# Thirty-odd steps of the first batch's attention moved in a written-out order, and four matmul groups of the MLP put behind others

## The chip, the cores and the metric

The kernel runs on one core of a Trainium2 chip. The metric is the device time in microseconds (us) of one execution. Three runs of the kernel before took 256.25, 258.79 and 259.25 us; their median is 258.79.

## The reference

Four batches, eight heads, 768 positions, head size 64; everything comes and goes in float32. Attention lets a position see the four first positions (sinks) and the last 128. Its output, heads side by side, is `x` (768 rows of 512), which goes through a ResMLP:

```python
keep = is_sink | in_window                  # 4 sinks, window of 128
a = softmax(where(keep, q @ k.T / 8, -1e9))
x = concat_heads(a @ v)                     # [4, 768, 512]
tok = einsum('ts,bsd->btd', w_tok, alpha1 * x + beta1)
u = x + lam * tok
ch = relu((alpha2 * u + beta2) @ w_ch1) @ w_ch2      # 512 -> 2048 -> 512
out = u + lam * ch
```

## The kernel before, in words

The program is one list of 1143 small steps ("tasks"). `Plan.add` (L44) records each while the code walks through the batches; `Plan.emit` (L54) then writes out the instructions in the order that the tuple `ORDER` (L216) gives, by task number. The string `ENGINES` (L282) gives each task's engine (0 ACT, 1 DVE, 2 PE, 3 POOL, 4 SP), `HOMES` (L297) gives each buffer its slot, and `IDLES` (L307) puts some matmuls on zeros ahead of a few early PE tasks. So an engine does its tasks in the order in which they stand in `ORDER`, and a task waits for the data that it reads and for its slots to be free.

Batch 0's attention. Queries and keys come as head pairs: pair 0 in float32, cast by DVE; pairs 1 to 3 by POOL loads that cast to float16 on the way (`load_qk`, L390). PE turns them round (L504, L507), ACT or DVE copies them to `qkT`. PE makes scores (L617, L681), ACT their exponentials `E` (L639, L686), POOL or a bias on PE masks them, PE multiplies with the values (L718), and DVE normalises (L743, L744) into `x`. For batch 0 POOL multiplies `x` with alpha1 · lam (L753) into `xh`, which PE contracts with the transposed w_tok (`wtokT`, made from loads in the first microseconds by L816, L809 and copies at L155/L157) in L849; DVE adds the sum to `x` (L856), ACT or POOL casts it to `u16` (L155, L157). `fold_rows` (L1164, L1166) makes the rows alpha1 · lam and beta1 · lam (a product, then a shuffle that spreads it over partitions). Before that POOL makes small constant tiles: the masks (L333 to L341), `bm` (L354, L358, one 8-column tile for the sinks), the identity `iden` (L325, L326), and the selector with an 8×8 identity (`make_sel`, L365, L369), which the transpose of the alpha2 and beta2 rows (`abT`, L1168) needs.

The MLP. `uTp` (L890) turns two column blocks of three `u16` tiles round into a PSUM bank, and ACT or DVE scales them into `uT` (L873, L876). A group (`mlp1`, L929) is four matmuls of 128x128 by 128x384: one of 16 column blocks of w_ch1 for one half (three row blocks) of the batch; its result sits in one of four PSUM banks `d` until a relu frees it (ACT L935, DVE L937). The second matmuls follow (L1114; batches 1 to 3 by a Strassen-like scheme, L1046). The attention of the next batch is spread between these groups.

The weights. w_ch1 comes as four quarters by POOL loads with a cast (`load_w1`, L448), of four column blocks each; a group needs its quarter. After the second quarter has landed, SP may go on: it issues a tiny "gate" copy (L455) that waits for the quarter, and the loads behind it are w_ch2 (L444), keys and queries of batch 1 (L397) and values (L407). ACT issues some of these loads too. POOL or DVE folds w_ch2 with lam (L831).

Batch 0's groups stand in this order on PE, by task number: groups of the quarters at hand, then the last quarter's groups of half 0 (291, 289, 293, 295), with the two transposes `uTp` of half 1 (246, 241) between them, then three groups of an earlier quarter (257, 277, 259), then 267 and on.

Of the kernel before, what the change touches and what calls it, by code (L numbers as in the profile page):

```python
# [77 lines left out]
def kernel(  # L78
# [119 lines left out]
    for r in range(NR):  # L198
# [18 lines left out]
        26, 6, 9, 7, 10, 5, 11, 8, 18, 15, 72, 19, 1, 12, 3, 0, 4, 2, 22, 14, 73, 74, 45, 48, 46,  # L217
        17, 39, 49, 47, 53, 13, 40, 50, 41, 90, 95, 43, 91, 51, 54, 103, 52, 16, 44, 61, 104, 42,
        96, 109, 100, 62, 107, 110, 63, 55, 28, 108, 92, 56, 101, 21, 68, 65, 59, 93, 20, 69, 97,
        102, 111, 94, 24, 98, 57, 60, 30, 112, 105, 23, 58, 99, 113, 128, 106, 114, 116, 25, 131,  # L220
        135, 78, 115, 64, 27, 138, 31, 32, 117, 132, 29, 129, 136, 33, 122, 66, 125, 34, 123, 137,
        119, 139, 126, 35, 79, 70, 120, 140, 124, 84, 71, 80, 133, 130, 141, 67, 146, 85, 134, 121,
        147, 144, 75, 118, 158, 86, 154, 148, 159, 145, 142, 87, 149, 150, 155, 160, 143, 76, 88,
        151, 156, 81, 77, 166, 152, 162, 167, 89, 127, 82, 163, 213, 83, 168, 209, 164, 165, 214,
        210, 153, 217, 179, 211, 178, 157, 197, 229, 36, 212, 215, 218, 185, 216, 226, 230, 219,
        176, 161, 177, 220, 169, 223, 222, 232, 225, 224, 221, 227, 237, 233, 279, 238, 234, 228,
        273, 280, 182, 171, 204, 291, 274, 175, 289, 292, 200, 231, 293, 290, 246, 294, 295, 199,
        384, 241, 248, 188, 186, 257, 296, 247, 172, 243, 277, 174, 181, 242, 259, 258, 187, 170,
        278, 267, 37, 260, 271, 358, 268, 198, 285, 349, 272, 381, 301, 286, 366, 351, 303, 302,
        189, 297, 378, 173, 304, 281, 180, 352, 203, 249, 190, 282, 298, 379, 250, 287, 380, 192,  # L230
        353, 385, 288, 206, 283, 386, 369, 375, 367, 265, 284, 368, 202, 370, 266, 363, 376, 371,
        253, 377, 201, 299, 254, 372, 364, 183, 382, 191, 300, 373, 615, 365, 275, 374, 383, 357,
        261, 276, 408, 262, 387, 263, 184, 409, 205, 195, 239, 411, 264, 410, 395, 269, 396, 240,
        397, 270, 196, 388, 614, 621, 235, 412, 400, 194, 244, 398, 236, 401, 255, 617, 251, 245,
        256, 389, 390, 399, 252, 311, 359, 207, 193, 391, 424, 616, 335, 425, 393, 341, 426, 392,
        336, 648, 427, 634, 413, 394, 312, 636, 414, 428, 419, 404, 420, 415, 360, 405, 313, 429,
        208, 422, 337, 416, 361, 441, 421, 622, 402, 314, 423, 442, 626, 403, 305, 638, 315, 406,
        430, 640, 316, 435, 431, 306, 641, 355, 436, 443, 619, 437, 338, 649, 618, 438, 362, 317,
        432, 637, 407, 307, 433, 345, 444, 339, 439, 635, 318, 445, 450, 434, 639, 644, 319, 451,
        628, 452, 620, 440, 308, 645, 340, 453, 417, 446, 323, 447, 418, 320, 309, 448, 324, 321,  # L240
        658, 322, 329, 449, 642, 659, 454, 325, 625, 643, 330, 646, 347, 455, 326, 623, 343, 647,
        464, 344, 456, 465, 348, 466, 460, 457, 467, 650, 327, 458, 331, 461, 629, 459, 472, 462,
        632, 463, 653, 356, 651, 656, 627, 332, 38, 654, 480, 333, 342, 624, 652, 473, 310, 476,
        468, 471, 470, 469, 481, 474, 488, 885, 477, 475, 482, 492, 655, 490, 493, 350, 483, 478,
        514, 491, 516, 489, 657, 479, 515, 660, 517, 630, 882, 665, 518, 663, 354, 328, 666, 502,
        880, 661, 664, 498, 879, 519, 508, 499, 346, 503, 678, 662, 512, 509, 679, 504, 513, 487,
        484, 671, 485, 676, 486, 506, 677, 877, 548, 505, 672, 680, 507, 526, 549, 546, 527, 631,
        334, 522, 674, 681, 528, 547, 907, 523, 534, 903, 529, 633, 682, 675, 878, 542, 683, 535,
        890, 689, 543, 550, 685, 684, 690, 510, 551, 494, 511, 673, 667, 544, 495, 668, 891, 496,
        686, 545, 901, 687, 669, 497, 693, 888, 688, 883, 530, 694, 670, 700, 531, 524, 897, 701,  # L250
        698, 500, 691, 525, 696, 699, 552, 501, 697, 704, 553, 558, 695, 705, 904, 692, 562, 559,
        706, 909, 887, 707, 563, 564, 898, 708, 702, 566, 565, 910, 715, 703, 567, 532, 716, 889,
        713, 533, 709, 714, 896, 520, 710, 556, 717, 521, 538, 557, 537, 540, 539, 536, 560, 541,
        899, 718, 921, 572, 922, 881, 711, 574, 884, 573, 576, 712, 561, 719, 902, 577, 575, 555,
        727, 720, 569, 908, 721, 580, 728, 578, 722, 581, 729, 554, 723, 905, 730, 568, 739, 724,
        579, 725, 592, 570, 911, 726, 582, 740, 593, 588, 912, 583, 595, 584, 571, 906, 743, 589,
        731, 585, 900, 590, 732, 605, 744, 587, 733, 596, 606, 734, 607, 611, 594, 597, 602, 745,
        612, 586, 613, 599, 895, 603, 591, 757, 765, 600, 758, 601, 759, 766, 741, 771, 760, 742,
        916, 772, 751, 917, 746, 773, 752, 913, 761, 919, 774, 886, 767, 918, 604, 762, 763, 598,
        768, 777, 764, 779, 920, 923, 780, 914, 755, 915, 778, 608, 756, 926, 930, 735, 609, 931,  # L260
        924, 927, 781, 736, 925, 775, 782, 737, 928, 753, 929, 893, 738, 934, 754, 892, 769, 935,
        932, 610, 941, 770, 819, 776, 942, 894, 939, 820, 821, 940, 937, 936, 823, 749, 822, 945,
        748, 824, 938, 747, 827, 933, 948, 950, 750, 952, 943, 951, 825, 953, 787, 828, 944, 807,
        788, 797, 826, 808, 949, 946, 829, 798, 801, 954, 830, 791, 802, 956, 947, 792, 783, 955,
        957, 963, 961, 784, 789, 958, 962, 811, 790, 964, 959, 785, 812, 965, 805, 786, 795, 806,
        960, 967, 796, 799, 793, 968, 966, 970, 972, 794, 813, 971, 969, 815, 973, 814, 809, 800,
        816, 803, 810, 974, 978, 804, 976, 979, 837, 975, 977, 835, 838, 980, 841, 836, 839, 842,
        818, 843, 840, 845, 981, 832, 982, 846, 817, 986, 844, 831, 990, 987, 983, 988, 847, 991,
        984, 851, 833, 992, 1002, 993, 834, 848, 855, 852, 985, 849, 1003, 859, 856, 1004, 989,
        1006, 850, 860, 1005, 853, 998, 1007, 1008, 868, 999, 857, 1009, 997, 865, 995, 858, 862,  # L270
        996, 869, 866, 1000, 874, 994, 854, 1001, 1016, 863, 875, 1040, 1017, 1038, 1041, 1032,
        1039, 871, 1020, 872, 1028, 1021, 1011, 1024, 1029, 1013, 1018, 1033, 1012, 1025, 1034,
        1019, 1036, 1010, 1035, 1042, 1037, 1076, 1043, 1070, 1077, 870, 1074, 1071, 1054, 1075,
        1022, 1055, 1060, 1023, 1048, 1061, 1058, 1049, 1066, 1059, 1014, 1044, 1015, 1067, 1072,
        1045, 1056, 1073, 1026, 1057, 1078, 1068, 1079, 1064, 1069, 1046, 1027, 1050, 1063, 1047,
        1052, 1082, 1053, 1051, 1084, 1083, 1062, 1065, 1030, 1085, 1080, 1101, 1031, 1081, 1091,
        1102, 1107, 1092, 1097, 1093, 1103, 864, 1108, 1105, 867, 1098, 1111, 1106, 1104, 1113,
        1112, 1089, 1114, 1115, 1086, 1116, 1090, 861, 1094, 1087, 1117, 1099, 1109, 1100, 1121,
        1095, 1110, 1125, 1118, 1122, 1124, 1134, 1126, 1123, 1128, 1135, 1127, 1119, 1136, 1088,
        1140, 1120, 873, 876, 1131, 1129, 1141, 1096, 1137, 1142, 1132, 1130, 1133, 1138, 1139,  # L280
    )
    ENGINES = (  # L282
        "3313134433443333444444444444444433334441111201201202120212021213030121211201211210200200"
        "2020201202011202020202020213213213213213213202002020202020213121312131213121312131404444"
        "4044413314433334411114413334444042213221321021020121021021321202020020211212021212120212"
        "1212020202120202120212020212020202020212122221022221422221022221422221022221013111111131"
        "1311333333302002002102132002132002102020101212010321213120301212131201012121312010121213"
        "1203212131212131213421342104110121042104213401012020202021202020212120202020212120202121"
        "2121202111202021202120202011202121212121111121212121212121132111213121421021421421421044"
# [1033 lines left out]
```

The softmax here doesn't subtract the row's maximum and nothing guards it: scores larger than these inputs give would overflow.

## Time and profile before

| what | value |
|---|---|
| runs (us) | 256.25, 258.79, 259.25; median 258.79 |
| span of the profiled execution | 254.3 us, 5499 instructions |
| PE busy | 245.6 us, 97% of the span |
| DVE, ACT, POOL busy | 190.7, 133.2, 103.2 us |
| mean granted clock of PE | 0.997 |
| w_ch1 quarters issued by POOL at | 20.96, 21.77, 22.50, 23.23 us |
| landed at | 30.52, 35.95, 39.15, 43.40 us |

All times within a run are counted from the start of the profiled span. In a list of waits each line says which engine and which instruction waited, for whom, the total, how many times and the longest. In a timeline a line is: start, duration, engine, source line, operation, output and inputs, number of instructions, and in brackets the idle time just before and what ended it. "PEld" is the loading of weights, and an engine's name with a "q" its issuing part. The chain of waits is followed back from the last instruction to the first.

### The profile page before, as it was taken

What the parts mean: (1) busy time and instruction counts of PE and PEld (TensorE: products, weight loads), DVE (VectorE), ACT (ScalarE), POOL (GpSimd) and SP (SyncE); (2) the same over time, 40 slices, a digit from 0 to 9 for tenths busy, and PEclk for the clock granted to TensorE, in tenths of its full rate; (3) what the DMA queues carried; (4) which work ended last, traced back from release to release, by engine and by line L of the source; (5) the groups of instructions that cost most, each with busy time, mean ns of one, the idle gap of its engine ahead of it and who ended that gap; (6) DMA issues with size and microseconds to landing.
All of it is one profiled execution on the core that took longest, in us unless ns stands there. A gap on an engine that the chain in (4) does not pass through costs nothing.

```text
span 254.3 us, 5499 instructions
## 1 busy us (share of the span) xinstructions
PE 245.6 (97%) x2167; PEld 159.9 (63%) x2167; DVE 190.7 (75%) x402; ACT 133.2 (52%) x219; POOL 103.2 (41%) x124
## 2 busy tenths in 40 slices
PE   7799997999999999999999999999999999999993
PEld 7554644666555544566687686667667676667882
DVE  5688986767888874978879995578778983228892
ACT  2599913879977034787833434566660235543000
POOL 8318845876455527515782040065662120000010
PEclk9999999999999999999999999999999999999998
DMA  6999999899999999998484764520000140100327
GB/s 182 205 215 266 272 269 316 246 377 300 221 158 233 234 208 156 195 249 180 110 170 107 128 122 138 144 65 0 3 0 3 30 84 13 41 0 3 117 73 268
DMA packets 86129, 38.79 MB, mean 153 GB/s; under 512 B 73540, under 2 KB 80460, under 8 KB 86104
## 3 DMA queue, kind: packets, MB, share of 16 engines
q1 hardware_dynamic: 66576, 28.06, 47.3%
q10 hardware_dynamic: 15784, 7.11, 11.8%
q0 software_dynamic: 3744, 3.28, 8.0%
q8 instruction: 17, 0.28, 0.4%
q14 instruction: 8, 0.07, 0.1%
HBM read 29.91 MB, written 6.29 MB: 142 GB/s over the span
## 4 chain that ended last, share of the span: by engine, by line
PE 84%; DMA 11%; DVE 2%; POOL 1%; SPq 0%; issue 0%
PE h L929 32%; PE P L1046 22%; PE tok L849 9%; PE ch L1114 8%; DMA w1f<-in_moe_w_ch_dram 8%; PE pv L718 3%; PE S L617 3%; DMA nat<-in_k_dram 3%; PE tp L507 1%; POOL w1f L448 1%; PE tp L504 1%; DVE qkT L157 1%; DVE E L696 1%; PE pv L711 1%; PE pv L604 1%; PE idle L148 0%
## 5 line engine op out<-in xcount | busy, mean ns | idle before, releaser
L929 PE MATMUL h<-uT,w1f 128*128 128x384 f16 x512 | 89.8, 326 | 1.5 <-DMA w1f<-in_moe_w_ch_dram 1.5
L929 PEld LDWEIGHTS <-w1f 128*128 128x128 f16 x512 | 48.2, 98 | 32.7 <-DMA w1f<-in_moe_w_ch_dram 1.9
L935 ACT ACTIVATE hT<-h 128x384 f16<-128x384 f32 x77 | 37.0, 491 | 39.5 <-PE h L929 39.3
L937 DVE TENSOR_SCALAR hT<-h 128x384 f16<-128x384 f32 x51 | 27.8, 555 | 23.4 <-PE h L929 22.8
L1046 PEld LDWEIGHTS <-hT 128*128 128x128 f16 x408 | 39.5, 98 | 6.7 <-issue 0.2
L639 ACT ACTIVATE E<-S 128x1024 f16<-128x1024 f32 (+1 forms) x39 | 38.1, 1001 | 7.6 <-PE S L617 6.3
L762 POOL TENSOR_TENSOR tm<-x,la_b 128x512 f32<-128x512 f32 x18 | 24.3, 1353 | 24.2 <-DVE x L744 12.3
L849 PE MATMUL tok<-xh,wtokT 128*128 128x512 f16 x144 | 33.0, 379 | 0.0
L1059 DVE TENSOR_TENSOR x<-x,P 128x256 f32<-128x256 f32 x45 | 18.3, 419 | 11.3 <-PE P L1046 10.2
L1046 PE MATMUL P<-w2f,hT 128*128 128x256 f16 x216 | 26.5, 273 | 0.0
L849 PEld LDWEIGHTS <-wtokT 128*128 128x128 f16 x144 | 13.9, 98 | 15.0
L1114 PE MATMUL ch<-w2f,hT 128*128 128x512 f16 x96 | 23.2, 379 | 0.0
L1046 PE MATMUL P<-w2s,hT 128*128 128x256 f16 x192 | 23.1, 273 | 0.0
L1082 POOL TENSOR_TENSOR x<-x,pt 128x256 f32<-128x256 f32 x4 | 3.4, 854 | 47.5 <-DVE pt L1077 47.5
L155 ACT CAST u<-x 128x512 f16<-128x512 f32 x15 | 9.2, 615 | 24.9 <-DVE x L856 24.3
L744 DVE TENSOR_TENSOR x<-pv,rec 128x256 f32<-128x256 f32 x48 | 20.4, 425 | 1.7
L155 ACT CAST n<-nat 128x768 f16<-128x768 f32 x21 | 16.9, 828 | 8.9 <-DVE x L1125 6.4
L718 PEld LDWEIGHTS <-E 128*128 128x128 f16 x328 | 14.8, 98 | 5.1 <-issue 1.1
L856 DVE TENSOR_TENSOR x<-x,tok 128x512 f32<-128x512 f32 x24 | 16.0, 683 | 2.3 <-PE tok L849 2.3
L718 PE MATMUL pv<-vfs,E 128*128 128x65 f16 x328 | 17.7, 194 | 0.0
L579 POOL TENSOR_SCALAR_AFFINE_SELECT E<-E 128x512 f16<-128x512 f16 x12 | 7.5, 648 | 20.6 <-ACT E L639 20.6
L743 DVE RECIPROCAL rec<-pv 128x4 f32<-128x4 f32 x48 | 8.6, 179 | 7.2 <-PE pv L718 6.9
(134 smaller groups left out, 340.6 us busy)
## 6 DMA issues: line engine op xcount, KB each, us to landing
wst_w<-in_moe_w_ch_dram SPq DMA_DIRECT2D x8, 512.0 KB, 8.2
nat<-in_q_dram SPq DMA_DIRECT2D x10, 384.0 KB, 3.9
vnat<-in_v_dram SPq DMA_DIRECT2D x14, 256.0 KB, 5.7
nat<-in_k_dram SPq DMA_DIRECT2D x8, 384.0 KB, 7.2
out_dram<-x SPq DMA_DIRECT2D x11, 256.0 KB, 3.1
out_dram<-x ACTq DMA_DIRECT2D x10, 256.0 KB, 3.7
wtn<-in_moe_w_tok_dram SPq DMA_DIRECT2D x6, 384.0 KB, 4.1
w1f<-in_moe_w_ch_dram POOLq DMA_DIRECT2D x4, 512.0 KB, 15.4
```

The costliest lines, as they stand in the source:

```text
L155: nc.scalar.copy(o, i)
L639: nc.scalar.activation(eT.t, pS.t[:, :, 0 : n * w].rearrange("p e (i w) -> p e i w", i=n), AF.Exp, scale=scale)
L718: nc.tensor.matmul(po.t[:, hl, :], eT.t[:, e_, off + i, c : c + P], vf[j][:, h, :], start=(r < 2 and n == 0), stop=(n == len(parts) - 1 an ...
L744: nc.vector.tensor_mul(bx.t[:, 4 * G : 4 * G + 4, :], po.t[:, :, 0:D], rec.t.to_broadcast([P, 4, D]))
L762: engine[e].tensor_mul(bt.t, bx.t.rearrange("p h d -> p (h d)"), la1_b)
L849: nc.tensor.matmul(pt.t, wtokT[:, si, ti * P : (ti + 1) * P], hs[si].t, start=(si == 0), stop=(si == NR - 1))
L929: nc.tensor.matmul(ph.t, w1f[:, c, fi * P : (fi + 1) * P], bu.t[:, c, chk * NTOK : (chk + 1) * NTOK], start=(c == 0), stop=(c == NC - 1))
L935: nc.scalar.activation(bh.t[:, fi, :], ph.t, AF.Relu)
L937: nc.vector.tensor_scalar_max(bh.t[:, fi, :], ph.t, 0.0)
L1046: nc.tensor.matmul(pc.t, hh[:, nt * P : (nt + 1) * P], w(fi), start=(first and n_ == 0), stop=(n_ == HF - 1), skip_group_check=True)
L1059: nc.vector.tensor_add(row(bx)[:, cols], row(bx)[:, cols], pc.t)
L1114: nc.tensor.matmul(pc.t, bh.t[:, fi, nt * P : (nt + 1) * P], w2f[:, fi, :], start=(fi == 0), stop=(fi == NF - 1))
```

## The change

Only the three tables are touched (and a line break in `IDLES`), so the tasks and what each computes stay as they are.

The order. On PE the last quarter's groups of half 0 now stand behind the two `uTp` and behind the three groups that stood after: 257, 277, 259, 246, 241, 295, 291, 293, 289, 267. In batch 0's attention some thirty tasks are moved by a few places: on POOL `bm` (3) and the identity (0) stand ahead of the first load with a cast (9), the selector (5) and the product of the beta row (41) between the fourth and the fifth of these loads; on PE one transpose group (53) goes ahead of another (49), and scores, sinks and value products swap with neighbours; DVE's normalisations, shuffles and casts swap likewise. Among the loads of the list of steps that SP issues the order is the same. On ACT the load of batch 1's keys of pair 0 (171) now stands ahead of a relu (258) and a cast (231), which with relu 260 and two `uT` evictions (243, 242) come after it; before, a relu (238) and a cast (228) stood ahead of it. Later some twenty single tasks trade places with neighbours.

The engines. From DVE to POOL: the product 41, one w_ch2 fold (194) and an add (718). From ACT to POOL: the casts 228 and 372. From ACT to DVE: 44, 50, 83, 86 (copies of `abT`, one query-key block and two `wtokT` blocks) and the relus 238, 278, 286, 292, 503, 551. From DVE to ACT: 62, 258, 290, 468.

The slots. Some w_ch2 loads, batch 1 keys and values, PSUM banks and `E` tiles sit in other slots of the same kind. For instance the w_ch2 block 12 goes to slot 1 of the staging tiles rather than 0.

The diff, cut to the rows with the early tasks, the last quarter, and those of the engines and slots (the rows of `ORDER` are broken differently, so the two sides are to be read as running lists):

```diff
     ORDER = (
-        26, 6, 9, 7, 10, 5, 11, 8, 18, 15, 72, 19, 1, 12, 3, 0, 4, 2, 22, 14, 73, 74, 45, 48, 46,
-        17, 39, 49, 47, 53, 13, 40, 50, 41, 90, 95, 43, 91, 51, 54, 103, 52, 16, 44, 61, 104, 42,
-        96, 109, 100, 62, 107, 110, 63, 55, 28, 108, 92, 56, 101, 21, 68, 65, 59, 93, 20, 69, 97,
+        26, 6, 3, 7, 0, 10, 9, 11, 18, 8, 72, 15, 1, 19, 73, 12, 22, 45, 17, 41, 4, 2, 5,
+        46, 16, 14, 47, 74, 48, 53, 39, 13, 49, 54, 50, 43, 28, 42, 90, 95, 91, 51, 40, 103,
+        52, 61, 104, 63, 44, 96, 109, 21, 100, 62, 20, 107, 110, 24, 30, 55, 108, 101, 23,
...
-        176, 161, 177, 220, 169, 223, 222, 232, 225, 224, 221, 227, 237, 233, 279, 238, 234, 228,
-        273, 280, 182, 171, 204, 291, 274, 175, 289, 292, 200, 231, 293, 290, 246, 294, 295, 199,
-        384, 241, 248, 188, 186, 257, 296, 247, 172, 243, 277, 174, 181, 242, 259, 258, 187, 170,
-        278, 267, 37, 260, 271, 358, 268, 198, 285, 349, 272, 381, 301, 286, 366, 351, 303, 302,
+        161, 204, 223, 222, 175, 232, 225, 224, 221, 227, 171, 237, 233, 228, 279, 238, 234,
+        273, 280, 182, 257, 274, 186, 172, 277, 200, 258, 231, 259, 278, 174, 246, 199, 260,
+        241, 188, 384, 248, 295, 247, 291, 181, 170, 296, 187, 37, 243, 293, 292, 242, 198,
+        289, 267, 358, 349, 290, 294, 351, 271, 381, 268, 285, 272, 366, 301, 173, 189, 286,
...
     ENGINES = (
-        "3313134433443333444444444444444433334441111201201202120212021213030121211201211211210200200"
+        "3313134433443333444444444444444433334441131211201212120212021203030121211201211210210210"
...
     HOMES = (
-        "471305760131011000102123203130202001333101040201500112130053316501813134100210a010022031"
-        "5011400001101201106367453322030011213032113023012132032032203212110303321023113113130113"
+        "471305760131011000002123203130202021333101040201500112130153206501813134100211a013022001"
+        "5011400011000001136057453322003111223033113223012102032032203212113003321023113113103113"
```

## The prediction, put on record before the kernel was run

> **What bounds the kernel now.** I read the page's busy list first, then TensorE's waits, the chain that ended last, and the timelines of the engines around the one late wait.
>
> ```profile
> PE 245.6 (97%) x2167; PEld 159.9 (63%) x2167; DVE 190.7 (75%) x402; ACT 133.2 (52%) x219; POOL 103.2 (41%) x124
> ...
> PE h L929 <- DMA w1f<-in_moe_w_ch_dram: 1.5, 1, 1.5
> PE wT L809 <- POOL iden L326: 1.5, 1, 1.5
> PE idle L148 <- DVE warm L174: 1.1, 1, 1.1
> PE tp L507 <- DVE n L157: 0.3, 1, 0.3
> ```
>
> PE is busy 245.6 of 254.3 us; 8.7 us is all that fewer waits can give back, and the waits listed are 4.4 of it (the rest is the last stores' tail). A gain over 2% (5.2 us) is nearly out of reach; a loss needs a new stall.
>
> ```profile
> 1.72 7.26 DMA nat<-in_k_dram
> 20.27 0.74 POOL xh L753
> 21.01 2.22 POOL w1f L448 x3
> 23.23 20.17 DMA w1f<-in_moe_w_ch_dram
> 43.45 2.12 PE h L929 x12
> ```
>
> This is the chain's order of time: a key load, the first product `xh`, POOL's four issues of w_ch1, the landing of its last quarter, then PE to the end. So the wait of 1.50 us before 43.45 is real, and what delays POOL's issue at 20.96 delays it.
>
> ```profile
> 39.83 2.11 PE L929 MATMUL h<-uT,w1f 128*128 128x384 f16 x12
> 43.45 2.12 PE L929 MATMUL h<-uT,w1f 128*128 128x384 f16 x12 [1.50 <-DMA w1f<-in_moe_w_ch_dram]
> 45.41 0.50 PE L890 MATMUL uTp<-iden,u 128*128 128x128 f16 x6
> ...
> 36.82 0.40 SPq L444 DMA_DIRECT2D wst_w<-in_moe_w_ch_dram  x1
> 38.28 3.56 SPq L397 DMA_DIRECT2D nat<-in_k_dram  x1
> ...
> 41.24 0.39 ACTq L397 DMA_DIRECT2D nat<-in_k_dram  x1
> 44.31 0.49 ACT L935 ACTIVATE hT<-h 128x384 f16<-128x384 f32 x1 [2.57 <-PE h L929]
> 44.70 0.61 ACT L155 CAST u<-x 128x512 f16<-128x512 f32 x1
> 45.99 0.82 ACT L155 CAST n<-nat 128x768 f16<-128x768 f32 x1
> ```
>
> PE does three groups of twelve matmuls in all, stands for the last quarter, does three of its groups, and only then the transposes `uTp`. ACT stands idle in the same hole. From 43.45 to 250 PE waits for nothing.
>
> **What the Trainium skill says.** "DMA: Bandwidth & Descriptors", section "Issuing engines are not separate DMA queues": all issuers share 16 engines. The trace agrees: the DMA share of the stretches up to 100 us is 0.98 to 1.17, so issuing earlier moves landings less than one for one. Same page, "Why a DMA increments its semaphore by 16 and not by 1": only the full count says landed, and two loads in flight can't share one semaphore. I read from it that an issue on a reused semaphore first waits for the load that used it; the trace of before shows no such wait on ACT's issue at 41.24. "TensorE: Matmul & The Clock Gate", section "Architectural detail: the array is 16× 32×32, not 1× 128×128": PE pulls only weight loads ahead; the others are first in, first out. The trace agrees: the ready `uTp` at 45.41 stood behind the wait. "Perfetto Trace Analysis", "DMA Instruction — SWDGE (GPSIMD)": a POOL load's bar is descriptor making; here 0.72 to 0.77 us a bar against 9.6 to 20.2 to landing for w_ch1.
>
> **The change part by part.** The span of the profiled execution is 254.3; the runs are 256.25, 258.79 and 259.25, so 4.5 us lie between it and the median. I sum on the span and add 4.5.
>
> *The late wait.* Before: 3 groups, 3 last-quarter groups, `uTp`, one last-quarter group, `uTp`, then three third-quarter groups. After: 6 groups that need no last quarter, both `uTp`, then the four last-quarter groups. The same ten groups and two `uTp` end at 48.68 before (in the run of matmuls from 46.73), 47.18 without the wait. A group is 0.65 (1.30 per 8 matmuls), `uTp` 0.34. The last quarter is now needed 3 × 0.65 + 2 × 0.34 = 2.63 us of work later, which covers the 1.50. Alone: about −1.5.
>
> *What is late next.* The first `uTp` needs `u16` of row block 4 and a PSUM bank that the relu of group 4 frees. Both are ACT's, and in ACT's new order they stand behind the load of batch 1's key block 0 (L397); before, it stood after one relu and one cast more (41.24). The built program's semaphores show that this issue now waits for the landing of the w_ch2 load (L444) that SP issued at 36.82: same semaphore, since the order of SP's and ACT's loads changed. Before, it waited for a load of the first microseconds. It landed at 44.14 in the trace (POOL's product at L831 was released then). So ACT stands from about 39.9 to 44.15, then issues (0.40), does relu (0.39 until the next) and cast (0.61): 45.6. PE, six groups after 39.85, is ready at 43.75, and stands 1.85. Then two `uTp` (0.68) to 46.3 and four groups (2.6): 48.9 against 48.68: **+0.2**. Queued behind ACT's wait: two relus, cast `u16` 4, a cast of a key, and two `uT` evictions; PE's transposes wait for the first ones, DVE's other two evictions follow at 0.43 each and don't come last. The unknown is the landing: if the L444 load lands at 42.2 or before, nothing is lost and the whole −1.5 stays; break-even is 43.9; each us later than 44.14 costs one.
>
> *POOL's front.* The head mask `bm` and the identity (0.97 by POOL's timeline: 0.44 and 0.53) move ahead of the first cast-load. Issues at 1.31, 2.95, 3.70, 5.79, 7.50 and 9.87 become about 2.3, 3.4, 4.2, 6.3, then about 10 and 11: between the fourth and the last two now stands the product of the beta row with lambda (DVE 0.67; POOL 1.27 by L765's row) and the selector (0.73), and the product needs rows that landed by 9.2. So the first load is 1.0 late (landed 9.16), the next three 0.5, the last two 1.0 to 3. The identity's early end removes PE's 1.5 wait at 7.60, but the first `n` cast's data (chain: nat at 8.98) binds there: worth nothing on the path. PE's transposes of the first cast-loaded key come ahead of a ready one and see +0.5 to +1.0. I take +0.8 for the first scores, +0.65 to +1.0 for the first `xh`, so for w_ch1's issue at 20.96. Bounds: 0 (idle matmuls and DVE's gaps of 0.7 absorb it) to +2.5 (the last query load arrives 3 late, and its transposes, which lead to the first `xh`, with it).
>
> *Where that shift goes.* Later w_ch1 issues make the second quarter (35.95) land later, hence SP's gate and w_ch2's L444 load, 44.14, with full DMA engines by half to the whole of the shift: **+0.4 to +1.0**, I take +0.5. PE's own delay hides in its 1.85 stall.
>
> *Engine swaps.* DVE takes two `wtokT` evictions (0.55 each), one `qkT` (0.96), six relus (0.56); gives up the product, three casts or sums. ACT loses 8 operations and gains 4. ACT was busy 11.10 of 11.40 us in 20–31.4, DVE 10.28: about 1.6 goes from the fuller to the emptier, at most −0.5, taken as 0 since PE is 11.34 of 11.40 busy there. POOL takes four operations (casts 0.62 to 1.07, products 1.27) in stretches where it is busy 28.4 of 51.3 or less: hidden; without cover about 1.3 for the batch 1 cast.
>
> *Buffers.* Loads of w_ch2 and batch 1's keys change slots; SP's stand of 3.56 at 38.28 and the following wait until 46.19 shorten by 3 to 4 us. SP order is equal. PE waits for none of these before; hidden, 0 (earlier loads may delay the last quarter: it has 2.4 us of room to 46.3).
>
> *Small swaps after 48.7.* Same work with PE full: 0 ± 0.2.
>
> Sum: −1.5 + 1.7 + 0.5 + 0 = **+0.7**: span 255.0, time **259.5**.
>
> **Rivals.**
> (A) The wait changes its place, as above: +0.1 to +1.5, 258.9 to 260.3. For: the built wait; against: the landing time is of one execution.
> (B) The new wait is hidden: the L444 load lands by 42.2 since SP's and POOL's transfers reorder. Then −1.5 + 0 to +0.5 of early shift: 257.3 to 258.3. For: SP's gates thin out in that stretch; against: DMA share 1.17 there.
> (C) Slower: POOL's product waits for the lambda rows, and the last query and key loads, issued 3 late, hold PE's transposes, the first norm and with it L448. They landed at 15.27 and 16.56, and PE took up their transposes (L504) at 16.62 and 17.84: it decides once they land over 1.3 later. 3.0 late less 1.3 gives +1.7, all 3.0 without that room, and A's 0.2 and the 0.5 of shifted landing on top: 261.0 to 262.8. For: POOL is in order, and the chain runs through it; against: the rows were there at 9.2, before POOL gets to them.
> (D) The early part gets faster: B's −1.5, and of the identity's 1.5 between 0.5 and all: 255.8 to 256.8. Against: the chain starts at a load that isn't moved.
> (E) A stall over 5 us elsewhere, such as batch 1's cast on POOL: over 264.
>
> **How the numbers follow.** A 0.50, B 0.18, C 0.20, D 0.07, E 0.05. The range 256.6 to 262.6 leaves out most of D, E and the ends of C: about 2 in 10. A's own range is 258.9 to 260.3. Two per cent is about what a measurement of this kernel tells from no change: under 253.6 only D's far end, 0.05; over 264.0 E and a C grown beyond its range, 0.10; between, 0.85.
>
> **What would show it.** In PE's waits: no `h <- w1f` of 1.5, instead `uTp` L890 (five lines lower now) waiting some 1.9 near 44 for ACT's `u`. ACT idle some 4 us before a load L397 or relu, ended by `wst_w`. POOL's w_ch1 issues near 21.7. If ACT goes through at 41, B holds; if w_ch1 goes out after 23, C; if it goes out before 20.5, D. A median below 257 or above 262 makes the step of the landing, or of POOL's front, wrong.

## The result, and the profile after

The changed kernel takes 258.3 us in the median (256.88 to 260.3, 22 runs) against 258.01 (255.64 to 263.55, 22 runs) before on the same chip: ratio 1.0034, 95% interval 1.001 to 1.0058, so by the ratio about 0.9 us slower (the medians themselves differ by 0.3). 259.5 was forecast, +0.7. The measured 258.3 lies under rival A's own 258.9 to 260.3 and at the upper end of B's range. The profiled execution of after has a span of 256.4 us (its own time 258.09), against 254.3 (256.25) before. The profile of before was thus of one of its quicker executions, and the two traces differ by 2.0 us. In the later series of runs about a third of those of before had a mean granted clock of 0.993 or less and took about 3 us longer (medians 259.4 to 259.8 us against 256.5 to 256.8), while every trace but that of undo_718 (0.990) was taken at 0.997 or more, so small differences are read from the traces.

This is PE's list of waits after the change, without the one for the first matmuls, which stays. Those for `w1f` and for the identity are gone; six small ones stand in their place:

```profile
PE tp L512 <- ACT wtokT L155: 1.0, 1, 1.0
PE P L1051 <- DVE hS L992: 0.8, 1, 0.8
PE pv L723 <- DVE x L749: 0.6, 1, 0.6
PE vsp L573 <- ACT vfs L155: 0.4, 1, 0.4
PE S L686 <- DVE qkT L157: 0.2, 1, 0.2
PE tp L509 <- DMA n<-in_k_dram: 0.2, 1, 0.2
```

(After has line numbers five higher from `ORDER` on; the experiments have those of before.) At the place of the late wait PE's timeline shows 24 matmuls without a stop, then both `uTp`, then the next groups, with no wait in brackets:

```profile
41.43 4.06 PE L934 MATMUL h<-uT,w1f 128*128 128x384 f16 x24
45.33 0.83 PE L895 MATMUL uTp<-iden,u 128*128 128x128 f16 x12
46.00 6.18 PE L934 MATMUL h<-uT,w1f 128*128 128x384 f16 x37
```

The chain of waits, in order of time, no longer goes through w_ch1. It goes through the landing of the beta row, the selector step that stands behind POOL's product of that row, the last load with a cast, PE's transposes of it, and POOL's last products `xh`:

```profile
3.57 3.56 DMA lb_b<-in_moe_beta_dram
...
9.36 0.58 POOL sel L370
...
11.18 7.76 DMA n<-in_k_dram
18.98 0.53 PE tp L509 x12
...
30.70 3.93 POOL xh L758 x5
34.68 4.91 PE tok L854 x22
...
41.60 3.90 PE h L934 x24
```

That is the path of rival C: the last load landed at 18.94, 2.4 us later than before, and PE took up its transposes at 18.98 rather than 17.84.

ACT's load of the predicted wait went out at 42.23, and the relu behind it could follow at once when its matmuls were done. ACT's timeline:

```profile
42.23 0.40 ACTq L402 DMA_DIRECT2D nat<-in_k_dram  x1
44.30 0.49 ACT L940 ACTIVATE hT<-h 128x384 f16<-128x384 f32 x1 [2.77 <-PE h L934]
44.68 0.61 ACT L155 CAST u<-x 128x512 f16<-128x512 f32 x1
```

The start of the same PE task in both traces tells where the time went:

| PE task | before | after | difference |
|---|---|---|---|
| first scores (90) | 11.19 | 12.04 | +0.85 |
| first MLP group (237) | 39.83 | 41.43 | +1.60 |
| group behind the late wait (267) | 48.68 | 48.60 | −0.07 |
| second product `ch` (337), behind 72 us | 74.50 | 75.16 | +0.66 |
| first product with `hS` (572) | 135.72 | 137.38 | +1.66 |
| last product (1137) | 249.01 | 250.68 | +1.67 |
| end of the span | 254.3 | 256.4 | +2.0 |

So the early part lost 1.6, the missing late wait gave 1.67 back, two new stalls lost 0.73 and 0.91, small swaps 0.1, and the end 0.4. The move itself worked in full. What it gave was spent in the early part, and the two later stalls made the kernel slower.

### The profile page after: what moved, and what is told of

It is laid out like the page before. It is cut to its first block, busy times and chain, and to the rows that moved or that the text cites. A ratio compares the mean times of both kernels' runs of the same rounds, so it can differ in the third digit from the quotient of the medians.

```text
span 256.4 us, 5510 instructions
## 1 busy us (share of the span) xinstructions
PE 247.0 (96%) x2167; PEld 161.2 (63%) x2167; DVE 196.0 (76%) x405; ACT 129.5 (51%) x211; POOL 110.1 (43%) x129
## 4 chain that ended last, share of the span: by engine, by line
PE 84%; DVE 5%; DMA 4%; POOL 2%; issue 2%; ACT 1%; DVEq 0%; POOLq 0%; ACTq 0%
PE h L934 32%; PE P L1051 21%; PE tok L854 12%; PE ch L1119 7%; PE pv L723 4%; PE S L622 3%; DMA n<-in_k_dram 3%; POOL xh L758 2%; DVE hS L992 1%; DMA lb_b<-in_moe_beta_dram 1%; PE tp L512 1%; DVE w2f L836 1%; PE S L617 1%; PE pv L716 1%; DVE E L659 1%
## 5 line engine op out<-in xcount | busy, mean ns | idle before, releaser
L940 ACT ACTIVATE hT<-h 128x384 f16<-128x384 f32 x73 | 35.1, 491 | 40.9 <-PE h L934 40.6
L942 DVE TENSOR_SCALAR hT<-h 128x384 f16<-128x384 f32 x55 | 30.0, 555 | 21.2 <-PE h L934 20.1
L1051 PEld LDWEIGHTS <-hT 128*128 128x128 f16 x408 | 39.4, 98 | 6.8 <-issue 0.2
L767 POOL TENSOR_TENSOR tm<-x,la_b 128x512 f32<-128x512 f32 x18 | 24.9, 1384 | 22.4 <-DVE x L749 12.9
L854 PEld LDWEIGHTS <-wtokT 128*128 128x128 f16 x144 | 13.9, 98 | 15.3 <-issue 0.4
L155 ACT CAST u<-x 128x512 f16<-128x512 f32 x14 | 8.6, 615 | 26.2 <-DVE x L861 25.5
L155 ACT CAST n<-nat 128x768 f16<-128x768 f32 x20 | 16.2, 827 | 8.4 <-DMA nat<-in_q_dram 7.5
L1119 PEld LDWEIGHTS <-hT 128*128 128x128 f16 x96 | 8.6, 97 | 9.3 <-issue 0.4
```

The source lines that it names most:

```text
L155: nc.scalar.copy(o, i)
L767: engine[e].tensor_mul(bt.t, bx.t.rearrange("p h d -> p (h d)"), la1_b)
L854: nc.tensor.matmul(pt.t, wtokT[:, si, ti * P : (ti + 1) * P], hs[si].t, start=(si == 0), stop=(si == NR - 1))
L940: nc.scalar.activation(bh.t[:, fi, :], ph.t, AF.Relu)
L942: nc.vector.tensor_scalar_max(bh.t[:, fi, :], ph.t, 0.0)
L1051: nc.tensor.matmul(pc.t, hh[:, nt * P : (nt + 1) * P], w(fi), start=(first and n_ == 0), stop=(n_ == HF - 1), skip_group_check=True)
```

## The experiments

"Early" is `ORDER`'s first 99 tasks, "middle" the next 90, up to the first MLP groups. Both lists hold the same tasks in each of these stretches, so they can be exchanged whole, with their engines and slots (`E` and `rec` slots made to fit). Each trace is of one execution. How far two executions of the same code can lie apart, front_only and front_pe tell: they are the same up to the first MLP group, and PE reached it at 39.04 in one and 40.18 in the other.

**before_again.** No edit. 

> The kernel before, unchanged, for a second profile, since the first one is of an execution (256.25 us) 1.8 us under the median. Theory 1 (the changed order of the first loads moved the landings of w_ch1): the quarters land again near 30.5, 36.0, 39.2 and 43.4 us, PE waits 1.3 to 1.7 us for the last one, the span is 254 to 256.5. Theory 2 (the landings scatter from one execution to the next by 2 us and more): a quarter lands over 1 us from these times, the wait for the last one is under 1 or over 2 us. Whatever theory: if the span is near 256.3 the added time shows as a wait or a later landing that the first profile lacks.


Measured: span 254.1 (256.15 us), landings of the quarters 30.64, 36.17, 39.17, 43.16, the wait 1.4 us. Every PE task lies within 0.25 us of the first profile. So landings and the wait repeat, and theory 2 falls. The time again is near the low end of before's 59 runs (255.86; median 257.32); no profile here is of one of its longer executions.

**pe_only.** Before, with the move alone:

```diff
-  237,279,273, 291,289,293, 246, 295, 241, 257,277,259, 267   (PE's order)
+  237,279,273, 257,277,259, 246, 295, 241, 291,293,289, 267
```

(Their relus follow; 295 stays between the two `uTp`.) 

> The kernel before with the move of the last quarter's four groups alone (behind 257, 277, 259 and both transposes; their relus follow them, engines and loads as before). Theory 1: nothing queues behind a load on ACT here, the wait of 1.5 us vanishes, and 1.3 to 1.6 us are gained over before; the first profile's other stages stay. Theory 2 (the wait scatters with the landing): a gain between 0 and 2.5 us that is the wait of that execution, a median gain under 1. Rival 3 (a wait takes its place: half 1's casts come late): gain under 0.5 and PE waits before the transposes at L890.


Measured: 255.63 us, ratio 0.9928 (0.9898 to 0.9958). The timeline of PE:

```profile
39.48 4.06 PE L929 MATMUL h<-uT,w1f 128*128 128x384 f16 x24
43.38 0.50 PE L890 MATMUL uTp<-iden,u 128*128 128x128 f16 x6
43.75 0.82 PE L929 MATMUL h<-uT,w1f 128*128 128x384 f16 x4
44.41 0.50 PE L890 MATMUL uTp<-iden,u 128*128 128x128 f16 x6
```

The last quarter landed at 43.71, when PE was at `uTp`, so there was no wait, and task 1137 comes 1.80 us earlier than before. PE was 0.35 early at the first group already, ahead of the move, so the move itself gains 1.45, which is what its own sum said (1.5).

**head_new.** Before, with the changed early part. 

> The kernel before with the changed kernel's first 99 tasks only (POOL's front, early transposes, product on POOL), the rest in the old order and on the old engines. Theory 1: PE is 0.9 us late by the first scores and 1.2 to 1.6 us late at the first MLP group (41.0 to 41.4), POOL issues w_ch1 near 22.0, yet its last quarter lands at 41 to 42, so that the wait of 1.5 us is gone: the time stays within 0.3 us of before. Theory 2 (the landings scatter, the front only costs): last quarter at 43.5 to 45, time +0.8 to +1.6 us.


Measured: 255.89 us, 0.9945 (0.9918 to 0.9972): faster, which neither theory said. PE reaches the first group at 41.13 (+1.30), POOL issues w_ch1 at 22.13 (+1.17), yet the quarters land at 28.60, 31.12, 36.70 and 42.09. The wait is gone and task 1137 is 0.38 earlier. Theory 1's landings held; by the ratio its size was 1 us short, by the trace it fits nearly. The early loss shows in PE's waits: it stands for the 8×8 identity that the selector step makes, and on POOL that step now stands behind the product.

```profile
PE abT L1168 <- POOL iden L369: 1.1, 1, 1.1
```

**head_mid_old.** The changed kernel with the old early and middle parts. 

> The changed kernel with the old order, engines and slots for the first 189 tasks, so all up to the first MLP groups; the rest as changed. Theory 1: PE reaches the first MLP group at 39.8 again, w_ch1's second quarter lands near 36 again, so that ACT's load stands until a w_ch2 load has landed at about 44, PE's transposes of half 1 wait 1.5 to 2 us, and the two later stalls (0.7 us at 72, 0.9 us at 137) stay: 1.5 to 2 us slower than before in the profile. Theory 2: the early 1.6 us is gained and the wait is hidden, 0.8 to 1.5 us faster than the changed kernel.


Measured: 258.15 us, 1.005 (1.0025 to 1.0075). The premise of theory 1 was wrong: in this build ACT's load doesn't wait for the late w_ch2 load, and was issued at 39.21. PE gained 1.78 by 267 and lost it to the two later stalls and to a third, 1.2 us for batch 2's transposed queries near 98 us.

**head_old.** The changed kernel with the old early part only; here the wait of ACT's load for the w_ch2 load is in the build. 

> The changed kernel with the old first 99 tasks only, so with the built wait of ACT's load for a w_ch2 load, but with the old landings of w_ch1. Prediction's theory A: the second quarter lands near 36, the w_ch2 load behind its gate near 44, ACT stands until then, and PE waits 1.5 to 1.9 us before the transposes at L890; with the 1.7 us of the two later stalls the kernel is 1.5 to 2.5 us slower than before. Theory B (the wait is hidden even so): PE waits under 0.5 us there, and the time is that of the kernel with both early parts old, 0.3 to 1.3 us over before.


Measured: 259.1 us, 1.0112 (1.0042 to 1.0181; 6 runs). ACT's timeline and PE's:

```profile
44.03 0.46 ACTq L397 DMA_DIRECT2D nat<-in_k_dram  x1
44.59 0.49 ACT L935 ACTIVATE hT<-h 128x384 f16<-128x384 f32 x1 [3.71 <-PE h L929]
44.97 0.61 ACT L155 CAST u<-x 128x512 f16<-128x512 f32 x1
```

```profile
45.13 0.22 PE L890 MATMUL uTp<-iden,u 128*128 128x128 f16 x1 [0.27 <-ACT hT L935]
45.64 0.79 PE L890 MATMUL uTp<-iden,u 128*128 128x128 f16 x11 [0.29 <-ACT u L155]
```

The load went out at 44.03 (the prediction had 44.15), the relu and the cast followed, PE waited for them, and 267 began at 48.86 (the prediction had 48.9). PE's wait was only 0.56 instead of 1.85, because PE came 0.96 late to the first group. The bracket blames PE for ACT's idle time, but the relu's matmuls ended at about 43.55, half a microsecond before the load went out: the load queued ahead of the relu was the cause.

**front_only and product_sel.** Before, with one half each of POOL's early change:

```diff
-  9, 5, 8, 15, ... 12, 3, 0, 14, 13           (POOL; 3 = bm, 0 = identity)
+  3, 0, 9, 5, 8, 15, ... 12, 14, 13           (front_only)
```

```diff
-  9, 5, 8, 15, ... 12, 3, 0, 14, 13           (POOL; 5 = selector; 41 on DVE)
+  9, 8, 15, ... 12, 3, 0, 41, 5, 14, 13       (product_sel; 41 on POOL)
```

> The kernel before with only bm and the identity ahead of POOL's first load with a cast. Theory 1a (it is the first loads with a cast, 0.5 to 1.4 us later, that let SP's early loads land sooner and so w_ch1's quarters too): second quarter lands 2 us or more ahead of 36, last quarter 1 us or more ahead of 43.3, time -0.5 to -1.5 us. Theory 1b (it is the last two loads with a cast that count): landings stay within 1 us, PE's wait of 1.4 stays, time within 0.4 us.

> The kernel before with only the product of the beta row put on POOL, together with the selector, between the fourth and the fifth load with a cast. Theory 1b: the last two of these loads go out at about 10 and 11 us, PE stands about 1 us for the 8x8 identity at abT, w_ch1 goes out 1 us later yet its last quarter lands 1 us or more earlier than 43.3, net time 0 to -1 us. Theory 1a: w_ch1's quarters land later by 0.5 to 1 us, time +0.5 to +1.5 us.


Measured: front_only 255.81 us, 0.9898 (0.9838 to 0.9958; 6 runs); product_sel 257.74, 1.0007 (0.9976 to 1.0038). In front_only PE is 0.79 earlier at 237 and the second quarter lands at 33.19, but the last at 44.34, and PE waits 3.2 us in the profiled execution (257.05, the slowest of its runs). So theory 1a held for the second quarter and failed for the last. In product_sel the product waited for its rows and took long, as the source view of L1164 shows:

```profile
L1164 POOL TENSOR_TENSOR lb_b<-lb_b,lam_r x1: 1784/1784/1784, 9.9 to 9.9; 128x512 f32<-128x512 f32 x1
its engine sat idle before it (us, times) until:
  DMA lb_b<-in_moe_beta_dram: 3.0, 1
```

The last two loads with a cast went out at 12.30 and 13.06, PE is 1.33 late at 237, and w_ch1's last two quarters land at 40.05 and 44.85, 0.9 and 1.5 later than before. By its ratio product_sel loses nothing, by its trace 1.45 at task 1137; the runs don't settle which of the two is typical.

All fourteen traces together, those below too, tell what repeats and what scatters (us; PE at 237 as a difference from before):

| early part of POOL | traces | PE at 237 | second quarter lands | last quarter lands |
|---|---|---|---|---|
| old | before, before_again, head_mid_old, head_old, pe_only | −0.35 to +0.96 | 34.20 to 36.17 | 43.16 to 46.14 |
| `bm` and identity in front, product on DVE | front_only, front_pe, repaired, three_back | −0.79 to +0.51 | 31.48 to 34.46 | 42.19 to 44.81 |
| product on POOL and selector late | product_sel | +1.33 | 35.94 | 44.85 |
| both | head_new, after, undo_195, undo_718 | +1.30 to +1.94 | 30.00 to 31.12 | 40.29 to 42.09 |

So PE's early loss goes with the product on POOL, in all five traces that have it. That the front makes PE earlier is not shown, since front_pe, with the same early part as front_only, was 0.35 late. The second quarter lands earlier in every trace with the front, and soonest with both. The last quarter lands earliest with both, too, but there the border isn't sharp: repaired, with the front alone, comes to 42.19. (In three_back the selector is late as well.)

The front comes with earlier landings of SP's own loads: its second value load, issued at 3.7 to 4.0, lands at 8.7 to 12.7 us in the eight traces with the front and at 12.8 to 15.3 in the six without. That this frees the engines for w_ch1 is argued from these times, not shown. (SP's w_tok loads don't separate the two: the last is issued at 19.54 in pe_only, which has no front, and at 21.12 in three_back, which has it.)

**undo_195 and undo_718.** The changed kernel, with one task put back each: the DVE fold 195 sixteen places earlier in `ORDER`; the add 718 on DVE behind `hS`. 

> The changed kernel with one task moved: the first fold of w_ch2 block 10 on DVE (195) goes back from just ahead of the other fold (193) to a place some ten tasks earlier, behind the mask of a score tile. Theory 1 (two DVE folds in a row beside a POOL fold hold up the normalisations that free PE's banks near 70 us): PE's wait of 0.62 before a value product near 72 us goes and the time falls by 0.4 to 0.8 us against the changed kernel. Rival (PE's new order of value products and score groups there is the cause): the wait stays, time within 0.2 us.

> The changed kernel with one task back on DVE behind the second half of the difference hS, as before: the add that makes xh of row block 5 of batch 2 (718). Theory 1 (POOL's add runs beside DVE's two hS differences and slows them from 2.64 to 3.71 us in sum): the two take about 2.65 again, PE's wait of 0.75 to 0.9 us near 137 us goes, time -0.7 to -0.95 us. Rival (hS is late for another reason, or PE meets the next wait at once): the wait stays or moves, time within 0.3 us.


Measured: 258.05 us, 1.0000 (0.9972 to 1.0029), and 257.65, 1.0008 (0.998 to 1.0035), against 1.0034 for the whole change: the ratios point the right way, but their intervals overlap. The traces decide. First DVE, POOL and PE in after around 135 us, then DVE in undo_718:

```profile
133.62 3.71 DVE L992 TENSOR_TENSOR hS<-hT,hT 128x1536 f16<-128x1536 f16 x2
```

```profile
134.65 1.86 POOL L770 TENSOR_TENSOR xh<-tm,lb_b 128x512 f16<-128x512 f32 x1
```

```profile
137.38 1.92 PE L1051 MATMUL P<-w2f,hS 128*128 128x256 f16 x16 [0.75 <-DVE hS L992]
```

```profile
134.03 2.64 DVE L987 TENSOR_TENSOR hS<-hT,hT 128x1536 f16<-128x1536 f16 x2
136.59 0.68 DVE L765 TENSOR_TENSOR xh<-tm,lb_b 128x512 f16<-128x512 f32 x1
```

With the add beside them, two subtractions on DVE last 3.71 in sum, and POOL's add 1.86 instead of 1.27. With the add put back on DVE the subtractions last 2.64, and PE's wait of 0.75 is not in the list any more: shown. At 72 us the pair is DVE's fold of w_ch2 and POOL's. In after two folds stand in a row on DVE, and PE waits for the normalisation behind them:

```profile
68.33 2.37 DVE L836 TENSOR_TENSOR w2f<-wst_w,lam_b 128x512 f16<-128x512 f32 x2
```

```profile
67.83 1.72 POOL L836 TENSOR_TENSOR w2f<-wst_w,lam_b 128x512 f16<-128x512 f32 x1
```

```profile
71.91 0.42 PE L723 MATMUL pv<-vfs,E 128*128 128x65 f16 x8 [0.62 <-DVE x L749]
```

In undo_195 one fold is left there:

```profile
68.31 1.76 DVE L831 TENSOR_TENSOR w2f<-wst_w,lam_b 128x512 f16<-128x512 f32 x1
```

That fold still takes 1.76 beside POOL's, but PE's wait of 0.62 is gone, and PE is 0.6 ahead of after from 72 us to the end.

**three_back.** The changed kernel with both of these and the product 41 on DVE. 

> The changed kernel with its three tasks that went from DVE to POOL or beside it repaired: product 41 and add 718 on DVE again, fold 195 earlier; everything else as changed, ACT's wait for the w_ch2 load among it. Theory 1: PE is 1 to 2 us earlier at the first groups than in the changed kernel, both late stalls go, 1.5 to 3 us under the changed kernel. Theory A inside it: as PE is now earlier than the w_ch2 landing, 0.5 to 1.5 us of this come back as a wait before the transposes at L890, gain 1 to 2 us.


Measured: 255.51 us, 0.9942 (0.9917 to 0.9968), about 1% under the changed kernel: three small steps held back all its gain. PE reaches the first group 0.51 later than before rather than 1.60, with the selector still late. So most of the early loss fits the product alone, though one trace against three (+1.58 to +1.94) is all that tells it from the selector. No wait came before `uTp`: ACT's load went out at 41.60.

**front_pe and repaired.** Before with front_only and pe_only together; and front_only's front, the old middle, the changed rest with 195 and 718 put back. 

> The kernel before with the two parts that gained by themselves: bm and identity ahead of the first load with a cast, and the last quarter's four groups behind the others. If they add: PE reaches the first group at 39.0, the last quarter lands at 43.5 to 44.5 and is needed at about 43.7 to 44, so that a wait of 0 to 0.8 us is left; 1.8 to 2.8 us faster than before. If the front only shifts PE towards the same landing: the wait grows by what the front gains, and the time is that of the move of the groups alone, 1.8 us faster.

> The changed kernel without what cost it: the product back on DVE and the selector early as before, bm and identity in front, the old order up to the first groups (so ACT's load waits for nothing late), 718 back on DVE, 195 earlier. Theory 1 (the costs are the early product, the two late stalls and nothing else): about the gain of both parts, 1.5 to 2.8 us faster than before. Rival (the changed second half has a hidden wait for batch 2's transposed queries near 98 us, 1.2 us in the run with both early parts old): that wait of 1 to 1.5 us appears, and the gain is 0.5 to 1.5 us.


Measured: front_pe 254.32 us, 0.9888 (0.9839 to 0.9938; 6 runs), the best of all, and repaired 255.27, 0.9929 (0.9903 to 0.9955). Both beat both kernels. In front_pe the last quarter landed at 44.81 and left a wait of 0.28. Its interval overlaps that of pe_only, and its trace, of the slowest of its runs, has task 1137 0.88 earlier than before where that of pe_only has 1.80, so that the front adds anything is not shown. repaired has PE 2.33 ahead of before at 267, and loses 1.0 of it near 97 us, as its rival said:

```profile
95.24 0.50 PE L617 MATMUL S<-qkT 64*128 64x256 f16 x6
96.78 0.29 PE L617 MATMUL S<-qkT 64*128 64x256 f16 x2 [1.04 <-DMA qkT<-n]
```

## Why the prediction came out, point by point

- **The sum** was +0.7, the measured +0.9 by the ratio and +2.0 between the two traces. Its total came near by luck: several of its terms are wrong, and they cancel.
- **The late wait, −1.5:** right. pe_only shows 1.45 from the first group on, and no new wait.
- **What is late next, +1.7:** the mechanism is right, the size in this kernel is 0. In head_old ACT's load stands to 44.03 and 267 starts at 48.86. In after it went out at 42.23, at the bound up to which "nothing is lost", and the relu behind it had no input before about 44.2: rival B, in this stage. The step that failed is "Later w_ch1 issues make the second quarter (35.95) land later". POOL did issue that quarter 1.1 later, at 22.87, and it landed at 30.89 instead of 35.95: from issue to landing it took 8.0 us instead of 14.2. So SP's gate opened 5 us early. The w_ch2 load behind the gate gained only 1.9 of that: it was issued at 31.76 rather than 36.82 and had landed by about 42.2 rather than 44.14. The prediction treated the landing as issue time plus a queue that stays the same. It took what the Trainium skill says ("DMA: Bandwidth & Descriptors", section "Issuing engines are not separate DMA queues": all issuers share the engines) one way only: it asked what a later issue does to its own load, and not what later POOL loads do for SP's.
- **POOL's front, +0.8 to the first scores:** right (+0.85), and for w_ch1's issue right (+1.1). The issues forecast at about 2.3, 3.4, 4.2, 6.3, 10 and 11 came at 2.71, 3.61, 4.33, 6.41, 10.42 and 11.18. The last of these loads then bound PE by C's path. C's rule, 2.4 later less the 1.3 of room, gives 1.1, and its transposes came 1.14 later. **"PE's own delay hides in its 1.85 stall"** failed with the stall: +1.60 at the first group counts in full, and is what the missing wait pays for. The +0.5 for the shifted landing should have been this +1.6.
- **The identity's early end:** worth nothing in after, as said; PE's 1.5 wait went and PE then stood 1.0 before the next transposes.
- **Engine swaps, hidden at 0:** wrong. The cover was named (POOL "busy 28.4 of 51.3 or less"), but it counts only POOL's free time. What the added POOL work does to DVE beside it was never priced: +0.9 at 136 us by add 718, and 0.6 of the +0.73 at 72 us by two DVE folds in a row, moved there by the order, beside one on POOL. The row of before had the sign: DVE's L831 fold 0.68 to 1.10.
- **Small swaps, 0 ± 0.2:** 0.1 in the middle; from PE's last task to the end of the span after and the kernels with its second half take 5.6 to 5.8 us, those with the old 5.3, so 0.3 to 0.5 for the end. Which of its swaps does this stays open.
- **Sums and readings that were off:** B's own terms, −1.5 with 0 to +0.5, give 257.3 to 257.8 and not 258.3, and C's give 261.2 to 262.5. ACT gives up 12 operations; 8 is its net loss, 219 to 211. In before ACT's load stood behind the load of `lam` on its semaphore, which went out at 26.49, not in the first microseconds. POOL's bars for w_ch1 last 0.75 to 0.81 us.
- **The profile against the median:** the 4.5 us between span and median were not a constant. Each run lies 1.7 to 2.4 over its own span; the rest is that the profiled execution was a quick one.

## What to carry to other kernels

A move on the bounding engine should be tried alone before its neighbours are moved with it: the four groups alone gained 0.7%, and three small steps on other engines spent it. When work goes to POOL, price what DVE does at that moment, and which of the two will start first, not POOL's free time. A landing depends on more than its own issue: check what a step does to every queue's early loads before adding its delay to a late one.

## What the runs showed of the hardware

DVE and POOL slowed each other in these pairs: two subtractions of 128x1536 f16 from 2.64 to 3.71 us, POOL's add of 128x512 from 1.27 to 1.86, DVE's fold of 128x512 from 0.68 to 1.76, POOL's product of the same size from 1.27 to 1.78.

The traces also show which of the two pays: in the pairs below it was the one that started later. In before a subtraction that had started first kept its 0.95 us, and POOL's product behind it took 1.85:

```profile
187.83 0.95 DVE L987 TENSOR_TENSOR hS<-hT,hT 128x1536 f16<-128x1536 f16 x1
```

```profile
188.06 1.85 POOL L762 TENSOR_TENSOR tm<-x,la_b 128x512 f32<-128x512 f32 x1 [0.34 <-DVE x L744]
```

At 132.87 it was the other way round: POOL's product had started 0.32 earlier and kept its 1.27, and the subtraction took 1.77 (the next one, with nothing beside it, 0.94). So the 2.64 of before has one such delay in it already. In after the add 718 started within the first subtraction and took 1.86, and the second subtraction, which started within the add, took 2.02. Not every pair did this: POOL's 128x512 products and adds that started behind a DVE operation on a matmul result (`x<-pv,rec` or `x<-x,P`) took 1.26 to 1.27 in the traces of before, after, pe_only and the two undo runs.

And with POOL's first loads with a cast issued 0.6 to 2.9 us later, a load of 512 KB that POOL itself issued 1.1 us later landed 5 us earlier.
